# Twelve more calls of constant matmuls before the first output matmuls of a fused linear attention and expert kernel

## The chip, the cores and the metric

The kernel runs on one core of a Trainium2 chip. Its engines are TensorE (PE, matrix products), VectorE (DVE), ScalarE (ACT), GpSimd (POOL) and SyncE (SP, which here issues the DMA transfers). Each has a queue of its own that it works through in order, and they wait for each other by semaphores. The metric is the device time of one execution in microseconds (us), the median of several runs.

## The reference

The inputs are q, k, v (4 batches, 8 heads, 768 steps, 48 features) and a complex decay a for each step and feature. The first stage is a linear attention with a complex state:

```python
mag = np.sqrt(a_re * a_re + a_im * a_im)
scale = np.minimum(mag, 0.999) / (mag + 1e-06)
...
for t in range(S):
    new_re = ar * S_re - ai * S_im
    new_im = ar * S_im + ai * S_re
    S_re, S_im = (new_re + k[t] v[t]^T, new_im)
    y[:, :, t] = np.einsum('bhd,bhde->bhe', q[:, :, t], S_re)
```

The second stage takes y as x (768 steps of 384 features a batch) and runs four experts, each a causal softmax attention with 64 features and its own wq, wk, wv and wo. A gate x @ w_gate picks two of the four experts a step, and their outputs are added with softmax weights.

## The kernel before

**Linear attention.** The 768 steps of a batch are cut into 6 chunks of 128, taken two at a time (index k from 0 to 2), and the heads go in pairs (index g from 0 to 3). ACT, DVE and POOL first turn a into running magnitudes and angles by logarithms, scans, sines and exponentials (quotients, magnitudes, arcs, angles, sines, products; lines 518 to 580; tiles ab and qk). DMAs then move the features of each pair of heads into a tile fm (regroup, line 582). For each (b, g, k) three functions follow. head (line 613) transposes the keys on PE into pk, which ACT copies to kp, and forms the scores psc on PE, which DVE multiplies by the causal mask into kp. state (line 631) forms pu from kp and v and adds it to the running state tst, by DVE and ACT. tail (line 650) forms the outputs yu on PE, from kp and v (intra) and from tst and fm (inter). ACT then copies yu to x, or for g = 3 to yt, and DVE subtracts the rounding rest. The yt halves go to x by six DMAs.

**Experts.** moe(b) (line 687) makes the projections pp and pv of x, then the scores, softmax and outputs of a batch. The linear attention of batch b + 1 is issued in between.

**The order of the work.** Every operation of the program is first recorded, with a number, and then emitted in the order of the table ORDER (line 390). Each engine gets its operations chained in this order, so its queue is fixed. Before an operation whose number stands in the table WARM (line 273), the program emits matmuls on the constant tile src, which is all zeros: WARM gives the PSUM room that they write to, the number of calls n, and the width of a call's pieces. A width of 64 means two matmuls a call, one for each half of the output rows. Nothing reads their result. Before the change the first operation of the whole linear attention that PE works on (number 75, in head of batch 0) has 257 calls in front of it. The next entry is one call in front of number 173, and number 1218, the first pv projection of batch 0, has 43 calls 128 wide.

The emitting loop is where the change works:

```python
if i in WARM:
    room, n, width = WARM[i]
    x = self.ps.tile([128, 512], F32, name="warm", tag=room, bufs=1)
    for _ in range(n):
        for r in range(0, 128, width):
            chain("tensor", nc.tensor.matmul(x[r:r + width, :2 * C], real(self.warm[:, :width]),
                                             real(self.warm), start=True, stop=True))
```

Of the kernel before, what the change touches and what calls it, by code (L numbers as in the profile page):

```python
# [271 lines left out]
]  # L272
WARM = {
    75: ("psu_4", 257, 64), 173: ("psu_4", 1, 64), 230: ("psu_4", 3, 64), 1218: ("psu_4", 43, 128), 1311: ("psa_1", 1, 128), 1296: ("psa_1", 4,
    128), 840: ("psa_1", 19, 128), 852: ("psu_4", 3, 64), 830: ("psu_4", 12, 64), 870: ("psu_4", 10, 128), 884: ("psu_0", 2, 64), 897: ("psu_4",
    30, 64), 4702: ("psa_1", 2, 64),
# [79 lines left out]
class Work:  # L356
# [18 lines left out]
    def run(self):  # L375
# [14 lines left out]
        for i in order:  # L390
            engine, method, a, k = self.ops[i]
# [600 lines left out]
```

## Time and profile before

| | us |
|---|---|
| median of 3 runs | 440.46 |
| the three runs | 440.01, 440.46, 447.63 |
| the profiled execution's own time | 441.99 |
| span of its instructions | 440.2 |

All durations below come from the profiled execution, whose mean granted TensorE clock is 0.984 of full speed. Times in rows count from the first instruction. A row of the timeline merges equal instructions that follow each other: start, length, engine, line, operation, tiles, how often, and in brackets how long the engine was idle before and what released it. The lengths of merged matmul rows hold the drain of the last one, so neighbouring rows overlap a little.

### The profile page before, as it was taken

To read this page: it belongs to the slowest core of one execution; us is meant where nothing else is said; L and a number is where in the kernel's file an instruction comes from. 1 tells how busy PE (TensorE), PEld (TensorE's weight loads), DVE (VectorE), ACT (ScalarE), POOL (GpSimd) and SP (SyncE) were. 2 spreads that over 40 slices of the span, in tenths; PEclk is the share of its full clock that TensorE was granted. 3 is DMA by queue.
4 is the path that set the end of the run, shared out by engine and by line. 5 is a ranking of instruction groups with operands and counts; after the bars stand their busy time and mean duration, and the time that the engine had idled before them with its cause. 6 is when DMAs were issued, how large, how long until landed. Compare 5 with 4: busy or idle time off the path is not lost. (4 is left out here: it accounts for less than half of the span.)

```text
span 440.2 us, 12305 instructions
## 1 busy us (share of the span) xinstructions
PE 418.2 (95%) x4921; PEld 347.0 (79%) x4921; DVE 323.0 (73%) x752; ACT 331.2 (75%) x733; POOL 196.6 (45%) x184
## 2 busy tenths in 40 slices
PE   8997998999999899999999999989999999999996
PEld 8986886778877667788888777778787887887556
DVE  2797666799877898779998975977997724666522
ACT  6997798978699889879699989669485565335553
POOL 1352233254307467784136477383225446004780
PEclk9996799999999999999999999999999999999999
DMA  8934069625890752562659215770455011000103
GB/s 278 388 93 109 10 176 237 210 63 146 189 250 7 196 166 80 135 182 92 144 128 258 69 26 158 190 207 19 108 117 139 24 25 22 26 15 26 54 1 109
DMA packets 23545, 53.62 MB, mean 122 GB/s; under 512 B 3360, under 2 KB 9600, under 8 KB 23360
## 3 DMA queue, kind: packets, MB, share of 16 engines
q1 hardware_dynamic: 23488, 52.83, 43.5%
q8 instruction: 39, 0.64, 0.6%
q14 instruction: 18, 0.15, 0.1%
HBM read 26.74 MB, written 4.72 MB: 71 GB/s over the span
## 5 line engine op out<-in xcount | busy, mean ns | idle before, releaser
L405 POOL TENSOR_TENSOR pe<-pe 128x512 f32<-128x512 f32 (+2 forms) x62 | 82.3, 1329 | 25.4 <-PE po L405 15.4
L405 ACT ACTIVATE qk<-qk 128x768 f32<-128x768 f32 (+5 forms) x105 | 57.4, 566 | 4.5 <-DVE qk L405 3.9
L405 ACT ACTIVATE pe<-psS 128x512 f32<-128x512 f32 (+2 forms) x96 | 47.7, 542 | 15.1 <-PE psS L405 9.9
L405 PE MATMUL psc<-fm 96*64 96x128 f32 x768 | 52.8, 285 | 1.4 <-DMA fm<-qk 0.9
L405 POOL TENSOR_TENSOR qk<-qk 128x768 f32<-128x768 f32 (+2 forms) x24 | 35.7, 1500 | 38.7 <-ACT qk L405 38.7
L405 DVE CUSTOM_DVE_ANT_0 pm<-pm,mask 128x384 f32<-128x384 f32 (+4 forms) x96 | 46.7, 515 | 6.8 <-PE pm L405 6.4
L405 POOL TENSOR_TENSOR qk<-qk,ab 128x768 f32<-128x768 f32 (+2 forms) x19 | 28.5, 1504 | 48.6 <-issue 14.0
L405 PEld LDWEIGHTS psc<-fm 96*64 96x64 f32 x768 | 44.4, 142 | 5.8 <-DMA fm<-qk 1.4
L397 PE MATMUL warm<-src 128*64 128x256 bf16 (+1 forms) x697 | 47.1, 283 | 1.2 <-POOL src L405 1.2
L405 POOL TENSOR_SCALAR_AFFINE_SELECT pe<-pe 128x256 f32<-128x256 f32 x48 | 21.6, 467 | 59.3 <-ACT pe L405 56.5
L405 PE MATMUL psS<-qka 64*128 64x256 f32 (+3 forms) x480 | 47.6, 305 | 0.0
L405 PE MATMUL pp<-x,whi 128*128 128x256 f32 (+1 forms) x216 | 45.2, 327 | 1.1 <-DVE mx L405 0.3
L397 PEld LDWEIGHTS <-src 128*64 128x64 bf16 (+1 forms) x697 | 42.5, 114 | 3.4 <-POOL src L405 1.2
L405 DVE TENSOR_TENSOR qk<-qk,ab 128x768 f32<-128x768 f32 (+2 forms) x41 | 40.2, 993 | 6.6 <-POOL pe L405 1.8
L405 ACT ACTIVATE tst<-sum,fm 96x48 f32<-96x48 f32 x128 | 37.7, 327 | 9.1 <-DVE sum L405 8.7
L405 PE MATMUL po<-pe,v 128*64 128x256 f32 (+3 forms) x320 | 44.1, 396 | 0.0
L405 PEld LDWEIGHTS psS<-qka 64*128 64x128 f32 x480 | 37.6, 185 | 6.6 <-issue 2.6
L405 PE MATMUL yu<-kp,vt 128*64 128x128 f32 x384 | 37.3, 287 | 3.9 <-DVE kp L405 2.0
L405 DVE TENSOR_TENSOR kp<-psc,keep 128x512 f32<-128x512 f32 x48 | 32.6, 682 | 9.4 <-PE psc L405 9.0
L405 PEld LDWEIGHTS pp<-x,whi 128*128 128x128 f32 x216 | 32.5, 188 | 6.8 <-ACT v L405 0.9
L405 ACT ACTIVATE ab<-ab 128x768 f32<-128x768 f32 (+2 forms) x51 | 34.7, 689 | 2.3 <-DVE ab L405 1.8
L403 ACT ACT_TABLE_LOAD x27 | 34.6, 1283 | 1.2 <-PEq L981 0.8
(103 smaller groups left out, 913.8 us busy)
## 6 DMA issues: line engine op xcount, KB each, us to landing
fm<-qk SPq DMA_DIRECT2D x18, 578.2 KB
ab<-in_ak_dram SPq DMA_DIRECT2D x18, 384.0 KB
qk<-in_ak_dram SPq DMA_DIRECT2D x9, 768.0 KB
vt<-in_vk_dram SPq DMA_DIRECT2D x16, 384.0 KB
out_dram<-ob SPq DMA_DIRECT2D x24, 192.0 KB
fm<-qk SPq DMA_DIRECT2D x10, 385.5 KB
fm<-qk SPq DMA_DIRECT2D x16, 192.8 KB
x<-yt SPq DMA_DIRECT2D x72, 32.0 KB
```

What stands on the lines that cost most here:

```text
L397: chain("tensor", nc.tensor.matmul(x[r:r + width, :2 * C], real(self.warm[:, :width]), real(self.warm), start=True, stop=True))
L403: chain(engine, nc.scalar.preload_act_table_set(need))
L405: chain(engine, getattr(getattr(nc, engine), method)(*map(real, a), **{x: real(y) for x, y in k.items()}))
```

## The change

One entry is added to the table WARM: 12 calls of width 64, thus 24 matmuls on the constant tile, in front of operation 97. That is the first intra matmul of tail(0, 0, 0), the first output of the linear attention. They write to the room psu_4, which the 257 calls before them also used.

```diff
 WARM = {
+    97: ("psu_4", 12, 64),
     75: ("psu_4", 257, 64), 173: ("psu_4", 1, 64), 230: ("psu_4", 3, 64), 1218: ("psu_4", 43, 128), 1311: ("psa_1", 1, 128), 1296: ("psa_1", 4,
```

The entry stands on a line of its own, so every later line of the file has a number that is one higher. The queues of the other engines hold the same operations in the same order as before. On PE, this is the place before the change, at the end of the 257 calls (psc is head's scores, pk its transposes, yu the outputs, pu the state's update):

```order
L397 MATMUL warm<-src 64x256
L405 MATMUL psc<-fm 64x128 x8
L405 MATMUL pk<-ident,fm 128x96 x4
L405 MATMUL yu<-kp,vt 64x128 x4
L405 MATMUL pu<-vt,kp 64x48 x8
L405 MATMUL pk<-ident,fm 128x96 x4
```

And the same place with the change, where the line "..." stands for 23 more pairs of the two rows ahead of it:

```order
L398 MATMUL warm<-src 64x256
L406 MATMUL psc<-fm 64x128 x8
L406 MATMUL pk<-ident,fm 128x96 x4
L398 LDWEIGHTS src
L398 MATMUL warm<-src 64x256
...
L406 MATMUL yu<-kp,vt 64x128 x4
L406 MATMUL pu<-vt,kp 64x48 x8
L406 MATMUL pk<-ident,fm 128x96 x4
```

Between the transposes pk and the outputs yu, 24 weight loads and 24 matmuls have come in. A matmul of the program on 32-bit floats shows as two in the trace (psc, yu and pu), a transpose and a constant matmul as one.

## Rows read from the trace of the kernel before

**Rows 1.** The page's engine shares, and TensorE's granted clock in 40 slices.

```profile
PE 418.2 (95%) x4921; PEld 347.0 (79%) x4921; DVE 323.0 (73%) x752; ACT 331.2 (75%) x733; POOL 196.6 (45%) x184
...
PEclk9996799999999999999999999999999999999999
```

**Rows 2.** Busy time by window: length, each engine (instructions), clock, DMA share, GB/s.

```profile
34.55:36.58 2.03, 0.00 (x0) 0.00 (x0) 2.01 (x5) 2.03 (x5) 0.78 (x1) 1.00 0.74 180
36.58:36.95 0.37, 0.37 (x6) 0.37 (x8) 0.37 (x1) 0.37 (x2) 0.31 (x1) 1.00 1.05 250
36.95:50.60 13.65, 13.65 (x144) 12.37 (x142) 9.76 (x16) 8.00 (x21) 0.00 (x0) 0.50 0.15 44
```

**Rows 3.** Timeline of PE from 34 to 58 us.

```profile
34.00 0.55 PE L405 MATMUL pk<-ident,fm 96*128 96x96 f32 x4
36.58 0.82 PE L405 MATMUL yu<-kp,vt 128*64 128x128 f32 x8 [2.03 <-DVE kp L405]
...
39.71 3.66 PE L405 MATMUL psc<-fm 96*64 96x128 f32 x32
...
50.71 0.62 PE L405 MATMUL pu<-vt,kp 128*64 128x48 f32 x16
...
51.85 0.66 PE L405 MATMUL yu<-kp,vt 128*64 128x128 f32 x8 [0.19 <-DVE yt L405]
52.59 0.43 PE L405 MATMUL yu<-fm,tst 96*48 96x128 f32 x4
52.95 4.87 PE L397 MATMUL warm<-src 128*128 128x256 bf16 x43
```

**Rows 4.** The 257 calls by window, columns as in rows 2.

```profile
1.10:6.20 5.10, 5.04 (x48) 4.21 (x50) 1.23 (x8) 3.03 (x6) 1.00 (x4) 1.00 0.77 225
6.20:31.86 25.66, 25.66 (x470) 25.38 (x466) 19.23 (x37) 24.52 (x58) 8.71 (x9) 1.00 0.74 275
```

**Rows 5.** Timeline of PE in batch 1: score matmuls at full clock.

```profile
129.22 1.97 PE L405 MATMUL psc<-fm 96*64 96x128 f32 x32
```

**Rows 6.** Timeline of DVE: its idle times from 36.45 to 51.8 us.

```profile
38.84 0.25 DVE L405 TENSOR_TENSOR sum<-tst,pu 96x96 f32<-96x96 f32 x1 [0.21 <-ACT tst L405]
...
40.46 0.42 DVE L405 TENSOR_TENSOR x<-yu,x 128x256 fp32r<-128x256 f32 x1 [0.18 <-ACT x L405]
41.71 0.69 DVE L405 TENSOR_TENSOR kp<-psc,keep 128x512 f32<-128x512 f32 x1 [0.82 <-PE psc L405]
43.42 0.69 DVE L405 TENSOR_TENSOR kp<-psc,keep 128x512 f32<-128x512 f32 x1 [1.01 <-PE psc L405]
...
46.80 0.69 DVE L405 TENSOR_TENSOR kp<-psc,keep 128x512 f32<-128x512 f32 x1 [0.91 <-PE psc L405]
48.14 0.25 DVE L405 TENSOR_TENSOR sum<-tst,pu 96x96 f32<-96x96 f32 x1 [0.65 <-ACT tst L405]
...
51.37 0.42 DVE L405 TENSOR_TENSOR yt<-yu,yt 128x256 fp32r<-128x256 f32 x1 [0.86 <-ACT yt L405]
```

**Rows 7.** Waits of ACT, 36.67 to 53.5 us: total, times, longest.

```profile
ACT tst L405 <- PE pu L405: 3.0, 3, 1.9
ACT kp L405 <- PE pk L405: 2.2, 2, 1.9
ACT x L405 <- PE yu L405: 0.3, 1, 0.3
ACT yt L405 <- PE yu L405: 0.2, 1, 0.2
```

**Rows 8.** Timeline of SP, and a window of the loads of batch 1.

```profile
51.82 5.03 SPq L405 DMA_DIRECT2D x<-yt  x6
...
60.00:85.00 25.00, 22.82 (x313) 18.89 (x313) 17.72 (x43) 22.68 (x55) 8.60 (x7) 1.00 0.89 248
```

**Rows 9.** The two longest later gaps of PE, as windows.

```profile
131.40:132.60 1.20, 0.01 (x1) 0.00 (x0) 1.20 (x3) 1.20 (x4) 0.04 (x1) 1.00 0.58 144
295.85:297.25 1.40, 0.01 (x1) 0.00 (x0) 1.35 (x2) 0.62 (x1) 0.00 (x0) 1.00 0.25 97
```

## The prediction, made before the changed kernel ran

> **What bounds the kernel now.** I read the engine shares first: PE is busy for 95% of the span, no other engine for more than 75% [rows 1]. In a kernel of this kind the cost of one place is found by asking when PE is idle and when it is slow. The second row of the same group gives the slow part: TensorE's granted clock is at full level (2.4 GHz) in every slice but two, the fourth and fifth. The view of windows narrows it down [rows 2]: from 36.95 to 50.60 us, 13.65 us long, the clock is granted at one half (1.2 GHz), and PE is busy in all of it. This is the only such stretch between the kernel's start and its very end, and it accounts for the mean clock of 0.984 (0.5 of 13.65 us is 1.6% of 440.2).
>
> What did PE do before the clock fell? The timeline shows the transposes pk ending at 34.55, then nothing, then yu at 36.58: an idle gap of 2.03 us in which PE waits for DVE's kp [rows 3]. The clock falls 0.37 us after work resumes [rows 2]. The change puts its matmuls into exactly this gap.
>
> **What is added, and whether it fits.** Twelve calls of width 64 are 24 matmuls. The price is in the long row of the same kind: 470 in 25.66 us, or 54.6 ns each [rows 4], so 24 take 1.31 us. PE has nothing else queued before yu, so they run from 34.55 to about 35.86, and yu can still start at 36.58 when kp arrives. Direct cost: nothing, hidden by the wait for kp, with 0.7 us to spare. If the cover were thinner the other bound is the price of the first calls, 48 in 5.10 us, or 106 ns [rows 4]: 2.55 us, ending at 37.10 and delaying yu by 0.52. I take the low price, because the 470 and the score matmuls just ahead of the gap run at it, and the window of the gap still shows full clock. The room psu_4 is written by no other work between the 257 calls and these, so nothing is queued behind a wait for it; pk's readers on ACT wait for pk alone, and DVE, ACT, POOL and SP have unchanged queues.
>
> **What it may bring.** With the added work the idle gap shrinks from 2.03 to about 0.7 us. The trace has two longer ones after which the clock did not fall: 1.20 us at 131.4 and 1.40 us at 295.9, both with 1.00 granted afterwards as before [rows 9]. So I expect the clock to hold through 36.95. What is that worth? Three ceilings, one for each engine that takes part.
>
> PE: 13.65 us at half clock would be 6.83 at full, so at most 6.8 us. Single rows agree: 32 score matmuls take 3.66 us here [rows 3] and 1.97 at full clock [rows 5].
>
> ACT: its waits for PE between 36.67 and 53.5 add to 3.0 + 2.2 + 0.3 + 0.2 = 5.7 us [rows 7]. The rest is its own work, which TensorE's clock does not touch, so at most 5.7.
>
> DVE: its idle times up to the yt row add to 0.21 + 0.18 + 0.82 + 1.01 + 0.91 + 0.65 + 0.86 = 4.64 us [rows 6], each released by PE or by an ACT row that had itself waited for PE. DVE's own work does not get shorter, so yt cannot come more than 4.64 earlier.
>
> DVE has the lowest ceiling. Does it reach it? I walk along the three waits for scores. PE came to the 32 psc rows at 39.71; the rows ahead of them, 3.13 us, hold some 0.8 us that the lower clock added, so psc starts near 38.9 and its halves end at 39.9 and 40.9. DVE, without its idle 0.21 and 0.18 and the 0.82, is free for the first kp at about 40.5 and for the second at 41.2: both waits go. DVE reaches the third kp at 45.89 - 2.22 = 43.67. Eight transposes (1.1 us by the 0.55 of four [rows 3]) and 16 scores (1.0, half of rows 5) after 40.9, held up by the second kp until 41.9, end at 42.9, so that wait goes too. For sum, pu (0.62 at full clock [rows 3]) ends near 43.6 and ACT's tst near 44.0, against DVE free at 44.3. The yt row is tight: five rows of 0.66, 0.43, 0.62, 0.66 and 0.43 us [rows 3] with two short waits for ACT between them bring yu to about 46.3 and ACT's copy to 46.7, just when DVE is free. I therefore take 4.4 of the 4.64; the ends are 3.4 (1 us of new short waits on ACT and DVE) and 5.7 (ACT's ceiling, should DVE's rows overlap better than I can see).
>
> **Where it goes next.** After yt come six DMAs to x, issued from 51.82 [rows 8], just behind it; then 43 calls of constant matmuls on PE, 4.87 us at full clock in either case [rows 3]; then pv. All of these follow yt and move with it. The loads of batch 1 then keep the DMA engines 0.89 busy from 60 to 85 us [rows 8], but they are issued when buffers come free, by engines that are earlier by the same amount, and the DMA engines stand at 0.15 in the slow stretch [rows 2]. From there on PE is busy nearly throughout, and a queue that starts 4.4 us earlier ends 4.4 us earlier.
>
> **The sum.** The profiled execution took 441.99 us (span 440.2, 1.8 around it): - 4.4 + 0 gives 437.6, with a span of 435.8. That execution lies 1.5 above the median of the runs, 440.46, so the forecast on their scale is **436.1 us**, 1.0% faster.
>
> **Rivals.**
>
> 1. *The gap is not what costs the clock* (chance 0.08). The filler then runs in the gap, the clock falls at about 36.95 as before, and the time is 440.5. For it: the clock fell only after PE was at work again. Against it: no other gap of PE inside the kernel is as long, and no other is followed by a fall [rows 9]. The Trainium skill (TensorE: Matmul & The Clock Gate, section "Why this matters for your kernels") speaks on this side: it sets the idle gap that one has to avoid longer than the 2.03 us here. By that rule the change would bring nothing; the trace, in which the clock does fall after 2.03 us, does not agree.
>
> 2. *The fall is only put off* (0.10). At full clock PE finishes its small matmuls sooner and waits for DVE and ACT between them, some 2 us in all by the walk above (6.8 less 4.4 to 4.8). If the clock falls some microseconds later instead, a stretch like the old one follows, and it takes back what was won: 440.5, 1 us either way. Against it: from 60 to 85 us PE is 22.82 of 25 us busy, much of it the same attention rows, at full clock [rows 8].
>
> 3. *Slower: a new fall later on* (0.08). The place is the gap of 1.20 us at 131.4, where PE waits for DVE's kp [rows 9]. If PE is ahead there by its gain while DVE, busy with its own rows, is not, the gap grows; from about the 2.03 us that cost the clock here it decides. The price is up to 6.8 us (the half of 13.65), so 436.1 + 6.8 = 442.9. Against it: DVE should be as much ahead as PE, since it is the engine that sets the 4.4.
>
> 4. *The gain is lost to transfers* (0.06). If the loads between 60 and 85 us were bound by DMA alone, the start of batch 1's attention would not move and the 4.4 would turn into waits: 438 to 440.5.
>
> **How the numbers follow.** The forecast has the chance 0.68, with 434.8 to 437.1 for gains from 5.7 to 3.4. The range of 8 in 10 adds rivals 1 and 4 and the better half of 2: 434.7 to 440.8. Beyond 2% either way (under 431.7 or over 449.3, about what a measurement of this kernel can tell from no change) none of these cases reaches: 0.03 for faster, 0.03 for slower, for what I have not thought of, and 0.94 for within 2%.
>
> **What the profile of the changed kernel would show.** The 24 matmuls lie between pk and yu, end before 36.0, and yu still starts near 36.6, released by DVE's kp. The granted clock is 1.00 from 36.95 on, and the mean clock near 1.0. The 32 scores take about 2 us instead of 3.66. DVE's waits for psc are gone, PE has short waits for kp, tst and yt instead, and the six DMAs of yt start near 47.4 and the first pv near 53.2. The prediction is wrong if the clock still has a slow stretch of the same length, wherever it lies; if yt comes 4 us earlier but pv or batch 1's first transposes do not; or if the filler ends after kp.

## The result, and the profile after

| | us |
|---|---|
| the change, median of 20 runs | 437.77 (435.32 to 440.61) |
| the kernel before, measured beside it, 20 runs | 442.21 (439.14 to 451.18) |
| ratio, 95% interval | 0.9903 [0.9879, 0.9927] |
| profiled execution: own time, span | 438.5, 436.8 |

The change is 1.0% faster: 0.0097 of 442.2 is 4.3 us, where 4.4 was forecast. The absolute time is 1.7 us above the forecast of 436.1, because the kernel before took 442.2 beside it and not the 440.46 of its first three runs. The medians in us are over all runs; the ratios, their intervals and the times at half clock further on go by the runs within 1.5% of the fastest of the same kernel, which for the kernel before leaves out 4 of these 20.

The page of the changed kernel, engine shares and granted clock, beside [rows 1]:

```profile
PE 415.5 (95%) x4945; PEld 343.9 (79%) x4945; DVE 321.0 (73%) x752; ACT 331.5 (76%) x733; POOL 197.3 (45%) x184
...
PEclk9999999999999998999999999999999999999999
```

The 24 matmuls are there (4945 less 4921), and the dip in the fourth and fifth slice is gone. A small new one stands in the sixteenth; more of that below. The windows of the changed kernel, to set against [rows 2] (length, busy time of PE, PEld, DVE, ACT and POOL, clock, DMA share, GB/s):

```profile
35.43:36.35 0.92, 0.00 (x2) 0.00 (x1) 0.92 (x3) 0.92 (x3) 0.79 (x1) 1.00 0.77 199
36.35:36.95 0.60, 0.60 (x8) 0.41 (x8) 0.60 (x1) 0.60 (x3) 0.31 (x1) 1.00 0.94 195
36.95:50.60 13.65, 13.56 (x202) 11.13 (x201) 12.97 (x24) 12.65 (x33) 2.79 (x2) 1.00 0.19 53
```

Over the same 13.65 us the clock is 1.00 instead of 0.50, PE does 202 instructions instead of 144, and DVE is busy for 12.97 us instead of 9.76. PE's timeline of the changed kernel (start, length, engine, line, operation, tiles, count, idle time before and its releaser), beside [rows 3]:

```profile
33.45 0.55 PE L406 MATMUL pk<-ident,fm 96*128 96x96 f32 x4
33.93 1.50 PE L398 MATMUL warm<-src 128*64 128x256 bf16 x24
36.35 0.66 PE L406 MATMUL yu<-kp,vt 128*64 128x128 f32 x8 [0.92 <-DVE kp L406]
...
38.69 1.97 PE L406 MATMUL psc<-fm 96*64 96x128 f32 x32
...
46.44 0.66 PE L406 MATMUL yu<-kp,vt 128*64 128x128 f32 x8
47.19 0.43 PE L406 MATMUL yu<-fm,tst 96*48 96x128 f32 x4
47.55 4.87 PE L398 MATMUL warm<-src 128*128 128x256 bf16 x43
```

The filler ends at 35.43 and the idle gap has shrunk from 2.03 to 0.92 us. The 32 scores take 1.97 us, not 3.66, and the last yu starts 5.4 us earlier than in [rows 3]. DVE's timeline, beside [rows 6]:

```profile
36.21 1.00 DVE L406 SCALAR_TENSOR_TENSOR qk<-qk 128x512 f32<-128x512 f32 x1
37.13 1.27 DVE L406 TENSOR_TENSOR_SCAN ab<-col,carry,ab 128x512 f32<-128x512 f32 x1
38.33 0.22 DVE L406 TENSOR_TENSOR sum<-tst,pu 96x96 f32<-96x96 f32 x1
...
39.99 1.41 DVE L406 TENSOR_TENSOR kp<-psc,keep 128x512 f32<-128x512 f32 x2
...
43.09 0.68 DVE L406 TENSOR_TENSOR kp<-psc,keep 128x512 f32<-128x512 f32 x1
43.69 0.24 DVE L406 TENSOR_TENSOR sum<-tst,pu 96x96 f32<-96x96 f32 x1
...
45.97 0.41 DVE L406 TENSOR_TENSOR yt<-yu,yt 128x256 fp32r<-128x256 f32 x1
```

No row here has a bracket: all seven idle times of [rows 6] are gone, and yt starts at 45.97 instead of 51.37. DVE now works through this stretch without a break. PE's rows show no idle time behind the first yu either, but from there to the 43 calls they take 11.20 us. Before, the same rows took 16.37 us, 13.65 of them at half clock; with half of that off, 9.5 would be left. By this estimate PE waits some 1.7 us between its matmuls, and DVE sets the pace. Six DMAs of yt then start at 46.41.

### The profile page after: what moved, and what is told of

It is laid out like the page before. It is cut to its first block, busy times and chain, and to the rows that moved or that the text cites. A ratio compares the mean times of both kernels' runs of the same rounds, so it can differ in the third digit from the quotient of the medians.

```text
span 436.8 us, 12353 instructions
## 1 busy us (share of the span) xinstructions
PE 415.5 (95%) x4945; PEld 343.9 (79%) x4945; DVE 321.0 (73%) x752; ACT 331.5 (76%) x733; POOL 197.3 (45%) x184
## 5 line engine op out<-in xcount | busy, mean ns | idle before, releaser
L406 PE MATMUL psc<-fm 96*64 96x128 f32 x768 | 50.4, 276 | 1.5 <-DMA fm<-qk 1.0
L406 POOL TENSOR_TENSOR qk<-qk 128x768 f32<-128x768 f32 (+2 forms) x24 | 34.8, 1462 | 36.3 <-ACT qk L406 36.3
L406 POOL TENSOR_TENSOR qk<-qk,ab 128x768 f32<-128x768 f32 (+2 forms) x19 | 29.5, 1557 | 46.3 <-ACT qk L406 15.8
L406 PEld LDWEIGHTS psc<-fm 96*64 96x64 f32 x768 | 42.2, 136 | 5.9 <-DMA fm<-qk 1.6
L406 DVE TENSOR_TENSOR qk<-qk,ab 128x768 f32<-128x768 f32 (+2 forms) x41 | 39.3, 971 | 6.8 <-POOL pe L406 2.0
```

What stands on the lines that cost most here:

```text
L406: chain(engine, getattr(getattr(nc, engine), method)(*map(real, a), **{x: real(y) for x, y in k.items()}))
```

## The experiments

One measure serves in all of them. A run's **time at half clock** is worked out as (1 - mean granted clock) x 2 x span. The clock is on record to three decimals, so this time comes in steps of 0.9 us. Its median over the runs is 11.0, 12.3 and 10.6 us for the kernel before in three comparisons (beside e1 to e4, f1 to f4, and g1 to g3), and 0.9 for the change. Gains in us are one less the ratio, times 442.2.

**e3, thirty calls.** Does a gap closed altogether bring more?

```diff
+    97: ("psu_4", 30, 64),
```

> Thirty calls in the gap: 60 matmuls at 54.6 ns, 3.28 us, so yu starts near 37.8 instead of 36.6, 1.2 us after kp is there. Theory: the clock holds as with twelve, but the filler now lies on the path; DVE has some 0.3 to 0.8 us to spare against PE, so the kernel is 0.4 to 0.9 us slower than with twelve calls, 3.5 to 4 us faster than before. Rival (more filler is simply better, or its length does not matter because DVE sets the pace): as with twelve, 4.3 us faster than before.

Ratio 0.9909 [0.9870, 0.9948], 439.1 us; 3.5 us at half clock a run. PE's timeline:

```profile
34.02 3.47 PE L398 MATMUL warm<-src 128*64 128x256 bf16 x60
37.32 0.60 PE L406 MATMUL yu<-kp,vt 128*64 128x128 f32 x8
```

There is no idle time left, and yu starts 0.97 us later than in the change. The 43 calls begin at 48.28 instead of 47.55, so some 0.7 us are lost at this place; the interval (2.3 to 5.7 us won) is too wide to show it in the whole, or to tell the theory from its rival.

**e1, four calls.** A gap in between.

```diff
+    97: ("psu_4", 4, 64),
```

> Four calls in the gap instead of twelve: 8 matmuls at 54.6 ns, 0.44 us, so about 1.6 us of the 2.03 us gap stay idle in front of yu. Theory (the clock falls because PE idles too long in front of yu; the filler is worth what it shortens that gap): 1.6 us lies between the gap that cost the clock (2.03) and the ones that did not (1.40 and 1.20), so a smaller or no gain is expected: a slow stretch near 37 us in the profile, 13.65 us long, and 0 to 2 us faster than before in the median. Rival (a few dense matmuls on constants near the place are enough, however short): 4 us faster, as with twelve.

Ratio 0.9932 [0.9899, 0.9965], 439.68 us: 3.0 us won, above the 0 to 2 expected. First a row of PE's timeline, then (in a fence of its own) the window behind it:

```profile
36.90 1.12 PE L406 MATMUL yu<-kp,vt 128*64 128x128 f32 x8 [1.81 <-DVE kp L406]
```

```profile
36.40:43.20 6.80, 6.30 (x62) 5.77 (x64) 5.10 (x8) 5.25 (x11) 0.81 (x1) 0.50 0.34 87
```

The idle time was still 1.81 us and the clock fell, for 6.80 us and not 13.65. A single execution says little about this length: the one profiled in f4 below, with a gap of 2.16 us, was at half clock for 7.0 us in all. The median time at half clock, 7.0 us a run, lies between before and the change, as the gain does.

**e2, the twelve calls behind the gap.** The rival that what counts is the added matmuls, wherever they are, and not the gap.

```diff
-    75: ("psu_4", 257, 64), 173: ("psu_4", 1, 64), ...
+    75: ("psu_4", 257, 64), 173: ("psu_4", 13, 64), ...
```

> The same twelve calls, but behind the gap: in front of operation 173, where one call stood, there are now thirteen, so they run at about 39.5 us, after yu, pu and pk. Theory (the gap costs the clock): the gap of about 2 us stays, the clock falls near 37 us, and the 24 matmuls run at the half-clock price of 106 ns, 2.55 us in front of the 32 score matmuls, of which little is hidden. No gain from the gap; 0 to 2.5 us slower than before, less what the denser work may save by lifting the clock sooner. Rival (the extra matmuls help wherever they are, since it is dense work that keeps or lifts the clock): as fast as the changed kernel, 4 us under before.

Ratio 0.9984 [0.9946, 1.0022]: no gain. Time at half clock 10.6 us a run, as before. PE's timeline with the gap, the filler behind it and the scores, then the window at half clock:

```profile
36.38 0.66 PE L405 MATMUL yu<-kp,vt 128*64 128x128 f32 x8 [1.83 <-DVE kp L405]
...
39.05 2.42 PE L397 MATMUL warm<-src 128*64 128x256 bf16 x26
41.30 1.92 PE L405 MATMUL psc<-fm 96*64 96x128 f32 x32
```

```profile
37.35:40.75 3.40, 3.40 (x36) 2.83 (x34) 2.90 (x5) 2.62 (x7) 0.00 (x0) 0.50 0.45 139
```

The gap stayed and the clock fell behind it. In this execution it was back at 40.75, during the filler, and the scores ran at full clock. But the 2.42 us of filler now stood on PE's path, where the change hides them.

**e4, the gap closed by order, with no filler.** If the idle time is the cause, a shorter wait must do as well as a filled one. The first head's own operations that yu waits for, DVE's mask kp<-psc (83) and PE's transposes with ACT's copy (70 to 74), are put ahead of some rows of the magnitudes and products (DVE's, ACT's and POOL's), so that kp comes earlier. Nothing is added.

```diff
-    80, 81, 82, 299, 317, 159, 302, 318, 165, 307, 70, 71, 72, 73, 303, 83, 166, 319, 74, 167, 308, ...
+    80, 81, 82, 83, 299, 317, 159, 70, 71, 72, 73, 74, 302, 318, 165, 307, 303, 166, 319, 167, 308, ...
```

> No filler. Instead DVE does kp's product (83) before three other rows, at about 34.1 instead of 35.85, and ACT copies pk to kp (74) before three others, at about 35.1 instead of 36.67; each of the rows that they overtake gets 0.4 to 0.7 us later. PE then has yu near 34.9 and pu near 35.6, so no gap of 2 us is left. Theory (an idle PE costs the clock, not the lack of those matmuls): the clock stays at full level through 37 to 50 us and the kernel is 3 to 5.5 us faster than before. Rival (the constant matmuls themselves, dense and 128 rows deep, are what holds the clock): the slow stretch stays, and the gain is 0 to 1.5 us, what the earlier yu and pu give.

Ratio 0.9952 [0.9915, 0.9988], 438.57 us. The time at half clock fell from 11 to 2.2 us a run without one added matmul: it is PE's idle time here that costs the clock, and not a lack of constant matmuls. The gain, 2.1 us, is about half the change's and below the 3 to 5.5 expected. Where the rest went is open: in the profiled execution the overtaken rows of DVE start 1.0 to 1.1 us later than in before, but 0.8 of this was there ahead of them. The profiled execution is one of those that still lost the clock, and it shows why. Its PE timeline, then the window:

```profile
33.26 1.41 PE L405 MATMUL psc<-fm 96*64 96x128 f32 x16 [1.99 <-DMA fm<-qk]
```

```profile
35.75:42.55 6.80, 6.20 (x62) 5.41 (x60) 5.91 (x10) 6.25 (x13) 1.10 (x1) 0.50 0.48 123
```

The gap in front of yu is 0.31 us here, but fm's DMA landed late and left 1.99 us idle just ahead of it, as long as the old gap, and the clock fell.

**f4 and f3, DVE's work doubled** (operations 181 and 216, two kp rows of this stretch, emitted twice; the result is the same). The theory says that DVE has 4.6 us to spare here in before and none in the change. The rival is that DVE sets the pace in both.

```diff
-            chain(engine, getattr(getattr(nc, engine), method)(...))
+            for _ in range(2 if i in (181, 216) else 1):
+                chain(engine, getattr(getattr(nc, engine), method)(...))
```

On the kernel before:

> The same doubled DVE rows in the kernel before. Theory (before, PE at half clock sets the pace and DVE is idle for 4.6 us in this stretch): the 1.2 us go mostly into DVE's idle time, the kernel is 0 to 0.6 us slower than before, less than the change loses by them. Rival (DVE sets the pace in both): 1.0 to 1.3 us slower than before, as much as the change loses.

On the change:

> The change, with DVE's two products kp (operations 181 and 216) each done twice, which repeats a result: 2 x 0.61 = 1.2 us more of DVE's work at about 40 to 42 us. Theory (with the clock held, DVE sets the pace from 36 to 46 us: it has no idle time there): yt comes 1.2 us later than with the change, and the kernel is 1.0 to 1.3 us slower than the change, 3 us faster than before. Rival (PE or ACT sets the pace, DVE just keeps up): under 0.5 us slower than the change.

Before: ratio 1.0010 [0.9973, 1.0046], no loss that can be measured; but the interval, 1.2 us faster to 2.0 slower, still holds the rival's 1.0 to 1.3 us. The change: 0.9956 [0.9921, 0.9991] to before, so by the ratios 2.3 us of its 4.3 are gone (0.9956 - 0.9903; 1.5 against g3 below), more than expected, though the intervals overlap. The two runs point the way the theory says; they are not clear enough to exclude the rival. In the change with DVE's work doubled, DVE's row, the PE row behind it, and the window at half clock:

```profile
40.38 2.72 DVE L407 TENSOR_TENSOR kp<-psc,keep 128x512 f32<-128x512 f32 x4
```

```profile
43.25 1.71 PE L407 MATMUL psc<-fm 96*64 96x128 f32 x16 [0.85 <-DVE kp L407]
```

```profile
43.60:47.00 3.40, 3.40 (x46) 3.40 (x44) 2.63 (x6) 1.00 (x3) 0.00 (x0) 0.50 0.00 0
```

PE now waits for DVE, and in this execution the clock fell for 3.40 us behind the wait of 0.85. Part of the loss is thus DVE's own time and part the clock. The four runs at full clock throughout have a median of 437.6 us here and 436.6 in g3, which would put DVE's own part at 1.0 us, from few runs. yt came at 49.00, against 45.97; 0.4 us of this was there ahead of the stretch.

**f1 and g2, without the 257 calls.** Are the twelve worth something only because the 257 raised the clock ahead of them?

```diff
-    75: ("psu_4", 257, 64), ...
+    75: ("psu_4", 1, 64), ...
```

The kernel before without them:

> Before, with the 257 calls ahead of the first head cut to one; the gap at 34.5 us gets no filler. No engine but PE loses work, and PE has no real work before about 32 us. Theory (time is lost where real matmuls run at half clock): PE is cold from the start, so the first head (psc, pk; 1.4 us at full clock) and all up to 50 us run at half clock: 18 us instead of 14, and at 0.3 to 0.45 us lost for each us at half clock the kernel is 1 to 3 us slower than before. Rival (the clock of this stretch does not bound the kernel, the gain of the change came from elsewhere): the same time as before, though the slow stretch is longer.

Ratio 0.9988 [0.9946, 1.0029]: a miss. In before these 256 calls bring nothing that can be measured. Rows of PE's timeline show why:

```profile
32.64 2.00 PE L405 MATMUL psc<-fm 96*64 96x128 f32 x16 [31.05 <-DMA fm<-qk]
...
36.80 1.12 PE L405 MATMUL yu<-kp,vt 128*64 128x128 f32 x8 [1.33 <-DVE kp L405]
...
40.18 3.66 PE L405 MATMUL psc<-fm 96*64 96x128 f32 x32
```

The first head runs at the slow price too, but yu waits for DVE's kp anyway (1.33 us), and from there on the kernel before has lost its clock with or without them.

The change without them:

> The twelve calls in the gap without the 257 at the start (one left there). Theory (the filler can only hold a clock that is already up; f1 showed the rows from 32 to 51 us at half-clock prices without the 257): PE is at half clock when it meets the first head, twelve calls then take 2.55 us instead of 1.3, end near 37.5 and do not lift the clock at once: 0 to 1.5 us slower than before. Rival (the twelve calls are what counts, the 257 are not needed): 4 us faster than before, as the change.

Ratio 0.9946 [0.9918, 0.9975], 438.21 us: a gain of 2.4 us, where a loss of 0 to 1.5 was expected. PE's timeline, then the window:

```profile
35.30 2.77 PE L398 MATMUL warm<-src 128*64 128x256 bf16 x24
...
40.54 1.97 PE L406 MATMUL psc<-fm 96*64 96x128 f32 x32
```

```profile
39.05:50.60 11.55, 11.46 (x181) 9.22 (x180) 9.81 (x18) 10.39 (x29) 2.79 (x2) 1.00 0.03 8
```

The twelve calls start at the low clock (115 ns each, against 62 in the change) and the clock is full soon after them: the 32 scores take 1.97 us, not 3.66 as in f1. So the calls do not need a clock that is already up. The change with the 257 gains 1.0 us more in g3, which ran beside g2 (1.9 in its first comparison), but the intervals overlap.

**f2, g1 and g3, the later gaps.** The gaps at 131, 163 and 295 us filled too (numbers 884, 1639 and 2853; pu, pmr and pw). f2 adds 15 calls in front of 75 and writes the filler of 1639 and 2853 to the PSUM room of the operation that follows; g1 writes that of 2853 to another room, free by then; g3 is the change again, beside g1 and g2.

```diff
 f2:
+    97: ("psu_4", 12, 64),
+    75: ("psu_4", 272, 64), 1639: (None, 5, 64), 2853: (None, 8, 64), ... 884: ("psu_0", 9, 64), ...
+                room = room or f"{a[0].base.tag}_{a[0].base.room}"
 g1:
+    97: ("psu_4", 12, 64),
+    75: ("psu_4", 257, 64), 1639: ("psu_1", 5, 64), 2853: ("psa_0", 8, 64), ... 884: ("psu_0", 9, 64), ...
```

> The change, and filler in four more gaps: 15 more calls at the start (272, 0.8 us each 7.5 calls, over the wait of psc for its DMA), 9 instead of 2 in front of operation 884 (the pu gap near 131 us), 5 in front of 1639 (pmr near 163 us), 8 in front of 2853 (pw near 296 us). Each is shorter than the gap it fills. Theory (idle PE costs the clock, half clock costs time): the time at half clock inside the kernel goes from a median of about 1 us and up to 14 in single runs to nearly none; 0 to 1 us faster than the change, 4.3 to 5.3 faster than before, with less spread. Rival (the filler delays what is behind it in these places, where PE is the bound): 0.5 to 2 us slower than the change.

> As f2, but the filler ahead of pw (operation 2853) writes to the bank psa_0, which has long been free, instead of pw's own, and the 15 extra calls at the start are left out. In f2 the filler there waited for DVE's release of pw's bank and ran behind the gap of 1.46 us instead of in it, 1.06 us in front of pw. Theory (that filler is what f2 lost): the filler lies in the gap, pw is not delayed, and the kernel is 0.5 to 2 us faster than f2 and no slower than the change, 4 to 5 us faster than before. Rival (filler in the later gaps does not pay, wherever it writes, since the clock hardly falls there): as f2, about 2 us slower than the change.

> The change once more, beside the two others on the same chip: 4.3 us faster than before (ratio 0.988 to 0.993), with a median of some 1 us at half clock a run.

| | ratio to before | half clock, us a run |
|---|---|---|
| f2 | 0.9948 [0.9917, 0.9978] | 0.9 |
| g1 | 0.9930 [0.9889, 0.9971] | 0.0 |
| g3 | 0.9923 [0.9888, 0.9957] | 2.2 |

PE's timeline of f2 in front of pw, and then that of g1:

```profile
293.58 1.06 PE L399 MATMUL warm<-src 128*64 128x256 bf16 x16 [1.46 <-DVE qka L407]
294.71 0.45 PE L407 MATMUL pw<-whi,ot 128*128 128x384 f32 x1
```

```profile
292.06 1.06 PE L398 MATMUL warm<-src 128*64 128x256 bf16 x16
293.05 0.44 PE L406 MATMUL pw<-whi,ot 128*128 128x384 f32 x1
```

In f2 the filler inherited the wait for the room's release: the gap of 1.46 us stayed, and the filler ran behind it on PE's path. In g1 it runs in the gap. The gap was shorter there, because DVE's qka, which releases pw, ended at 292.76; so the filler still ran some 0.2 us past it. Expected were 0 to 1 us more than the change for f2, and 0.5 to 2 us more than f2 for g1. Against g3, f2 is 1.1 us behind and g1 0.3, within the intervals. Thus g1, with a median of nothing at half clock, is no faster than the change, and no kernel of the study beats it beyond its interval.

## Why the prediction was right

**The filler fits.** Forecast 1.31 us, end near 35.9, yu near 36.6; measured 1.50 with the drain, 35.43 and 36.35, released by DVE's kp. e3 shows the other side, yu 0.97 us late once the filler is longer than the wait.

**The gap is what costs the clock.** This was the step that the trace of before could not show, and rival 1 spoke against. e4 shows it: the wait shortened instead of filled, and the time at half clock falls from 11 to 2.2 us a run. e2 shows the reverse: the same filler, the gap left, no less time at half clock and no gain. Rival 2, a fall some microseconds later, did not happen in the profiled execution. But the gap's length alone does not decide. In the changed kernel the clock fell once more after a gap of 1.27 us at 163 us, where 1.20 and 1.40 in [rows 9] had cost nothing, and in f3 it fell after a wait of 0.85. A row of PE, then the window, from the changed kernel:

```profile
163.19 0.28 PE L406 MATMUL pmr<-ident,mx 128*16 128x128 f32 x1 [1.27 <-DVE mx L406]
```

```profile
165.20:168.60 3.40, 3.40 (x38) 2.71 (x33) 1.10 (x3) 2.39 (x7) 1.25 (x1) 0.50 0.58 186
```

In g2 the same wait stood in the same place, and the granted clock behind it is 1.00 (164.00 to 176.00):

```profile
164.73 0.28 PE L406 MATMUL pmr<-ident,mx 128*16 128x128 f32 x1 [1.26 <-DVE mx L406]
```

Eight of the profiled executions have this gap, at 1.25 to 1.27 us: the clock fell behind it in four (the change, g3, e2, f1) and held in four (e1, e4, f4, g2). One much longer gap cost nothing either, in f1, where the granted clock from 134.40 to 140.00 is 1.00:

```profile
134.33 0.67 PE L405 MATMUL pu<-vt,kp 128*64 128x48 f32 x16 [2.12 <-DMA vt<-in_vk_dram]
```

So a gap is a risk and not a threshold; what else enters stays open.

The fall at 163 us is rival 3's mechanism at a place that I had not named; the lead over before's rows went from 4.6 to 2.9 us there, a price of 1.7. The median of the change is 0.9 us at half clock, but 8 of its 20 runs, and 7 of the 12 of g3, have about 3.5 us or more: the large fall is gone from most runs, and smaller ones are left.

**The price is not half of 13.65.** Three ceilings were set, and the lowest, DVE's 4.64, named the right engine: its idle times all went, as walked through. yt came 5.40 us earlier. Of these 0.23 were there at 35 us already; the other 5.2 pass the ceiling by 0.5, because a row of DVE that follows without idle time starts about 0.07 us before the shown end of the row ahead (37.13 + 1.27 = 38.40, next start 38.33), and seven waits, each now closed, give about 7 x 0.07. f4 and f3 agree with the ceiling's cause, without showing it by themselves. The rows of the two profiled executions are what it rests on.

The runs of the kernel before show the price in another way. Its time at half clock differs from run to run, and its time goes with it: 0.33, 0.30 and 0.38 us for each us at half clock in the three comparisons (21 to 26 runs each, correlation 0.69 to 0.81). At none, the lines reach 436.7 to 438.1, around the change's own median. So 10 to 11 us less at half clock (10.6 to 12.3 less 0.9), at 0.30 to 0.38 each, go with 3 to 4 us. If PE alone set the pace, each would cost 0.5. These lines do not exclude that: they leave out the longest runs, which makes a line too flat, and through all runs but two (643 and 970 us) they give 0.43, 0.40 and 0.49. That the price was below half is seen in the rows of one pair of executions (5.2 us at yt for 13.65), not in these lines.

**Where it went next.** Six yt DMAs at 46.41 and pv at 52.17, forecast 47.4 and 53.2. Rival 4 had no part in this pair: the lead stayed between 5.4 and 5.9 us up to about 130. In the profiled execution of g3 PE did wait 2.08 us for the load of vt at 129.81, so other runs can lose time to transfers. At 163 us the gap of pmr and the fall behind it took 2.4, a wait of 1.01 us for DVE's kp at 199 went with another 1.2, and at 296 the change got 1.5 back. At the end 3.4 us were left between the two profiled executions; the runs say 4.3.

**What was luck.** The mechanism was right, but that 4.4 meets 4.3 so closely is in part chance. The lead at yt was 5.4 and not 4.4. The step "a queue that starts 4.4 us earlier ends 4.4 us earlier" did not hold in the pair of traces, where 2 us of the lead were lost after 130 us. And the sum priced one execution with 13.65 us at half clock, where the runs of before have medians of 10.6 to 12.3.

**Missed on the way.** I expected f1 to lose 1 to 3 us and g2 to win nothing. Both rested on one thought, that the 257 calls lend the gap's calls their clock. They do not need to: in g2 the clock rose behind the 24 matmuls without them.

## What to carry to other kernels

Look for the granted clock's dips, then for PE's idle gap ahead of each; a few matmuls on constants inside the gap, sized to end before the awaited tile arrives, are free there; elsewhere they stand on PE's path (2.42 us in e2, 1.06 in f2). They must write to a PSUM room that is already free at that point, or they take over the wait that they should fill. Price the regained clock by the engine that comes next, from its idle times in the slow stretch, not by half of the stretch; and once the largest gap is closed, filling smaller ones may bring nothing.

## What the runs showed of the hardware

**Two engines on one memory.** DVE and POOL slow each other, and at 294 us the one that started second took longer. In the kernel before:

```profile
294.22 1.56 POOL L405 TENSOR_TENSOR qk<-qk 128x768 f32<-128x768 f32 x1
```

```profile
294.24 2.36 DVE L405 SCALAR_TENSOR_TENSOR qk<-qk,ab 128x768 f32<-128x768 f32 x1 [0.57 <-ACT qk L405]
```

And in the change:

```profile
292.45 0.98 DVE L406 SCALAR_TENSOR_TENSOR qk<-qk,ab 128x768 f32<-128x768 f32 x1 [0.44 <-ACT qk L406]
```

```profile
292.57 2.28 POOL L406 TENSOR_TENSOR qk<-qk 128x768 f32<-128x768 f32 x1
```

With POOL 0.02 us ahead, DVE takes 2.36 us; with DVE 0.12 ahead, it takes 0.98 and POOL 2.28. The 1.40 us gap of [rows 9] at 295.9 was that: in the change it is absent. A race of about a tenth of a microsecond moves 1.4 us between two executions. The order of the starts is not the whole rule: at 168 us in before POOL's qk started 0.17 us ahead of DVE's (168.29 and 168.46), and it was POOL that took 2.52 us and DVE 0.94. The Trainium skill (GPSIMD Engine Reference, section "Specifications") states that GpSimd shares its SBUF interfaces with VectorE and contends with VectorE instructions that have two SBUF inputs, or run in a 2-port mode. These rows, a VectorE instruction with two such inputs, agree.

**What PE did before the clock rose.** In [rows 2] PE was busy for all of 13.65 us with the attention's small f32 matmuls and transposes, and the clock stayed at half. In e2 and g2 24 to 26 constant bf16 matmuls were followed by the full clock within 4 us of their start. That the kind of matmul decides is not shown: in e1 and e4 the clock rose after 6.80 us of the same f32 work, and in f3 after 3.40, with two constant matmuls in it at most.

**The clock's record has no entry ahead of its first event.** In f1 the 32 scores take 3.66 us, the price of half clock, in a stretch that the windows show as 1.00, because the first event in its record stands at 51.3 us. The price of a known row is the better witness there, as it was for the first 48 calls of [rows 4].
